# Attention over two heads of one batch per step, K and V in 32 KB runs, in a single-core decode block

## The chip, the cores and the metric

The kernel runs on one core of one Trainium2 chip. The metric is the time of one execution in microseconds of device time; a run is compared by the median of its executions. All data are float32. The whole program is one launch.

## What is computed

A transformer block for one decode step of a batch of two (B = 2, D = 512): a layer norm whose scale, shift and gate come from a condition vector, attention of 32 query heads over 8 cached key and value heads (Dh = 128), of which only the last W = 4096 positions count, and a feed-forward part (F = 1792). Cut to what matters:

```python
mod = (silu(c) @ w_mod).reshape(2, 6, 1, -1)       # six vectors: sa, ca, ga, sb, cb, gb
h = layernorm(x) * (1 + ca) + sa
q = (h @ wq).reshape(B, 1, 32, 128).transpose(0, 2, 1, 3)
k = repeat(k_cache[:, :, Sk - W:, :], 4, axis=1)    # W = 4096, Sk = 32768
v = repeat(v_cache[:, :, Sk - W:, :], 4, axis=1)
p = softmax(einsum("bhqd,bhkd->bhqk", q, k) * 128**-0.5)
o = einsum("bhqk,bhkd->bhqd", p, v)
x = x + ga * (o.transpose(0, 2, 1, 3).reshape(B, 1, 4096) @ wo)
h = layernorm(x) * (1 + cb) + sb
x = x + gb * (silu(h @ w1) @ w2)
```

All of it is read once: 67.1 MB of K and V, 8.4 MB each of wq and wo, 6.3 MB of w_mod, 3.7 MB each of w1 and w2.

## The kernel before

**Memory and loads.** All large data go through one ring in SBUF, `slots` (line 68): 8 slots of 16 KB in each of 128 partitions. `stream(n)` (line 70) hands out the next n neighbouring slots. Every large load is one DMA issued from SP, in the order of the program, and waits there until the slots' last readers are done and what they held has landed. w_mod takes three slots, wq four; then each head of one batch of K or V takes one (2 MiB, 16 KB to a partition), wo two, one and one, and the pieces of w1 and w2 one each. `load_k` and `load_v` (lines 77 and 84) put 32 neighbouring positions of a head into a partition.

**Start.** Matmuls with w_mod give the six vectors (lines 246 and 249), then h and its transpose, then q in two banks of PSUM (`q_ps`, lines 274 to 285), k outermost. Lines 286 to 305 spread q over `qbd`, the blocks that the scores use as weights: `qbd[0]` holds heads 0 to 3 of K, `qbd[1]` heads 4 to 7.

**Attention.** Step h (0 to 7, line 442) treats head h of both batches, with these stages:
- `fetch(h + 1)` issues K of head h + 1, then V of head h, two loads each.
- `keys(h, b, n4)` turns K by transposes of 32 x 32 blocks on VectorE, eight a step, into `kT` (two buffers).
- `scores(h)`: 16 matmuls into one bank, in row blocks by batch b and half c of the 32 positions in a partition; four row blocks of 32, accumulated over j.
- `maxima(h)`: the maximum of each row on VectorE, a matmul that turns the 128 maxima into one row, then the maximum per query head, written to `mrow`.
- `exponentials(h)`: a matmul with `mrow` (bank `bp`) makes the bias, ScalarE the exponentials `pr` and their sums `rowsum`.
- `turn(h)`: transposes `pr`, spreads it with the mask `group` (`zp`), four matmuls with `id4` (bank `pT`), and one ScalarE copy into `ptb`, two buffers of weights for V, with zeros between.
- `weighted(h, b)`: eight matmuls with V of batch b; after the second batch a copy to `ob`. `collect(h)`: four matmuls with `selh` that add the step's result into `o_all`.

`inorder` (line 314) fixes the order within each engine to that of the program. The loop's body (lines 442 to 460) is

```python
fetch(h + 1); keys(h, 0, 0)
turn(h - 1); collect(h - 2); weighted(h - 1, 0)
for n in range(1, 8): keys(h, n // 4, n % 4)
scores(h); maxima(h); exponentials(h)
weighted(h - 1, 1)
```

so V of a step is used one step later.

**End.** The sums are inverted, `o_all` is scaled and brought into `oTn` (lines 475 to 504), wo is applied as its parts land (`acc_o`, `ao`, lines 535 to 556), then the second norm, w1 (`hid`), the gate function and w2 (`acc_yw`, `acc_y`), and the result is stored. `busy` (line 521) issues matmuls into a bank that nobody reads, between these stages.

## Time and profile before

| | |
|---|---|
| median of 3 runs | 236.47 us (236.41 to 236.61) |
| the profiled execution, its own time | 236.49 us |
| its span, first to last instruction | 234.6 us |
| mean TensorE clock granted | 0.874 of full |
| read from HBM | 97.53 MB |
| ScalarE busy, GpSimd busy | 25.4 us, 10.3 us |
| loads of K, of V | 16 and 16, 2048.0 KB each |
| a load of K, of V, from issue to landing (median) | 26.3 us, 27.2 us |

How to read the profile's lines: in a group's line stand the source line, the engine (PE is TensorE, PEld its weight loads, DVE VectorE, ACT ScalarE, POOL GpSimd, SPq the issuing of DMAs from SyncE), the operation, what is written from what, the shapes and the count; then busy time, the mean of one in ns, and the idle time before them with what ended most of it. The time line lists the same by start and duration, with the idle time and what ended it in brackets. A windows row gives for a stretch its length, the busy time and count of PE, PEld, DVE, ACT and POOL, the granted TensorE clock, the DMA engines' busy share and GB/s. The DMA lines count packets, bytes and the share of 16 DMA engines' time that a queue's packets took. A float32 matmul of the program shows as two records. The chain of waits follows the work that ended last back from the end.

### The profile page before, as it was taken

How to read it: one execution, taken by the hardware profiler on the slowest of the kernel's cores; microseconds unless marked ns; L12 is line 12 of the kernel's file. 1: busy time of each engine (PE TensorE's matmuls, PEld its weight loads, DVE VectorE, ACT ScalarE, POOL GpSimd, SP SyncE). 2: the span in 40 equal slices, each digit the busy share in tenths (PEclk: the TensorE clock that was granted, in tenths of full speed). 3: DMA queues.
4: the chain of work that ended last, by engine and by line, in shares of the span. 5: the costliest groups of instructions: out<-in, count | busy, mean ns of one | idle time of the engine just before them, and what ended most of it. 6: DMA issues, size and time to landing. Idle time of an engine off the chain costs nothing.

```text
span 234.6 us, 2609 instructions
## 1 busy us (share of the span) xinstructions
PE 146.2 (62%) x1084; PEld 46.1 (20%) x1084; DVE 113.2 (48%) x175; ACT 25.4 (11%) x56; POOL 10.3 (4%) x30
## 2 busy tenths in 40 slices
PE   0006806917719767675775758746753968499894
PEld 0003201210101121121221112211211222226332
DVE  0124310179369389299398299397298050101130
ACT  2020000010030030030020030120030021003200
POOL 8600000010000000000000000000000000000000
PEclk9999975995965999999998897995995699769998
DMA  7998998999999999999999999999999999999991
GB/s 268 445 540 358 436 458 352 425 425 432 422 439 436 416 439 436 419 439 430 425 436 433 422 433 433 430 427 433 433 425 433 436 439 425 432 418 425 424 415 70
DMA packets 6527, 97.69 MB, mean 416 GB/s; under 512 B 732, under 2 KB 756, under 8 KB 1396
## 3 DMA queue, kind: packets, MB, share of 16 engines
q1 hardware_dynamic: 6492, 97.52, 97.5%
q8 instruction: 8, 0.13, 0.2%
q14 instruction: 3, 0.02, 0.0%
q10 hardware_dynamic: 24, 0.01, 0.0%
HBM read 97.53 MB, written 0.00 MB: 416 GB/s over the span
## 4 chain that ended last, share of the span: by engine, by line
DMA 47%; DVE 30%; PE 17%; ACT 3%; issue 1%; POOL 0%; SPq 0%; POOLq 0%
DVE kT L331 21%; DMA slots<-in_A_wq_dram 15%; DMA slots<-in_A_k_cache_dram 12%; DMA slots<-in_A_wo_dram 12%; PE s L343 8%; DMA slots<-in_B_w_dram 8%; PE q L279 4%; DVE zp L389 3%; PE acc_o L537 3%; DVE xp L387 2%; ACT pr L375 2%; DVE mx L353 1%; PE mT L355 1%; PE bp L371 1%; DVE qT L288 1%
## 5 line engine op out<-in xcount | busy, mean ns | idle before, releaser
L331 DVE STREAM_TRANSPOSE kT<-slots 128x1024 f32<-128x1024 f32 x64 | 73.7, 1210 | 0.3 <-DMA slots<-in_A_k_cache_dram 0.3
L343 PE MATMUL s<-kT,qbd 128*32 128x512 f32 x256 | 48.4, 668 | 13.5 <-DVE kT L331 13.5
L417 PE MATMUL o<-slots,ptb 128*32 128x512 f32 x256 | 37.3, 710 | 11.5 <-DMA slots<-in_A_v_cache_dram 11.0
L353 DVE TENSOR_REDUCE mx<-s 128x1 f32<-128x512 f32 x8 | 5.5, 691 | 36.1 <-PE s L343 36.1
L343 PEld LDWEIGHTS s<-kT,qbd 128*32 128x32 f32 x256 | 11.6, 124 | 51.2 <-DVE kT L331 28.5
L279 PE MATMUL q<-slots,hq_T 128*32 128x512 f32 x64 | 9.4, 756 | 9.1 <-DMA slots<-in_A_wq_dram 9.1
L396 PE MATMUL pT<-zp,id 128*32 128x256 f32 x64 | 5.6, 418 | 13.0 <-DVE zp L389 13.0
L417 PEld LDWEIGHTS o<-slots,ptb 128*32 128x32 f32 x256 | 7.9, 120 | 26.5 <-issue 24.2
L373 ACT COPY bias<-bp 128x1 f32<-128x1 f32 x8 | 1.3, 159 | 107.9 <-PE bp L371 107.9
L213 PE MATMUL mean_a<-mv_a,avg 128*128 128x1 f32 x2 | 0.6, 362 | 18.9 <-DVE avg L118 18.9
L389 DVE TENSOR_TENSOR zp<-xp,group 128x1024 f32<-128x1024 f32 x8 | 9.8, 1225 | 0.2
L537 PE MATMUL acc_o<-slots,oTn 128*32 128x512 f32 x48 | 8.0, 834 | 2.5 <-DMA slots<-in_A_wo_dram 2.5
L288 DVE STREAM_TRANSPOSE qT<-q 128x512 f32<-128x512 f32 x2 | 1.4, 718 | 16.3 <-PE q L279 16.0
L524 PE MATMUL junk<-selh,id 128*32 128x256 f32 x36 | 8.9, 380 | 0.0
L387 DVE STREAM_TRANSPOSE xp<-pr 128x512 f32<-128x512 f32 x8 | 5.7, 711 | 4.7 <-ACT pr L375 4.7
L565 DVE STREAM_TRANSPOSE aoT<-ao 128x128 f32<-128x128 f32 x1 | 0.3, 317 | 14.4 <-PE ao L548 14.4
L355 PE MATMUL mT<-ident,mx 128*1 128x128 f32 x16 | 3.0, 270 | 6.3 <-DVE mx L353 6.3
L432 PE MATMUL o_all<-ob,selh 128*64 128x128 f32 x64 | 5.3, 285 | 1.1 <-ACT ob L426 1.1
L426 ACT COPY ob<-o 128x512 f32<-128x512 f32 x8 | 4.7, 586 | 10.6 <-PE o L417 10.6
L279 PEld LDWEIGHTS q<-slots,hq_T 128*32 128x32 f32 x64 | 2.6, 134 | 16.0 <-issue 16.0
L371 PE MATMUL bp<-negscale,mrow 1*128 1x1 f32 x16 | 3.0, 256 | 4.2 <-DVE mrow L364 4.2
L249 PE MATMUL m_sp<-slots,scT 128*32 128x512 f32 x32 | 5.5, 780 | 0.0
(131 smaller groups left out, 94.0 us busy)
## 6 DMA issues: line engine op xcount, KB each, us to landing
slots<-in_A_k_cache_dram SPq DMA_DIRECT2D x16, 2048.0 KB, 26.3
slots<-in_A_v_cache_dram SPq DMA_DIRECT2D x16, 2048.0 KB, 27.2
slots<-in_w_mod_dram SPq DMA_DIRECT2D x1, 6144.0 KB, 17.2
slots<-in_A_wo_dram SPq DMA_DIRECT2D x1, 4096.0 KB, 27.3
slots<-in_A_wo_dram SPq DMA_DIRECT2D x2, 2048.0 KB, 29.0
slots<-in_B_w_dram SPq DMA_DIRECT2D x2, 1024.0 KB, 21.1
slots<-in_B_w_dram SPq DMA_DIRECT2D x1, 1792.0 KB
slots<-in_B_w_dram SPq DMA_DIRECT2D x2, 896.0 KB, 24.7
```

The costliest lines, as they stand in the source:

```text
L249: nc.tensor.matmul(m_sp[r, :], scT[:, k, :], cd[:, g], start=(k == 0), stop=(k == 3))
L279: nc.tensor.matmul(q_ps[n][32 * g : 32 * g + 32, :], hq_T[:, k, :], wv[:, n, g], start=(k == 0), stop=(k == 3),)
L331: inorder(nc.vector.transpose(kT[h, b][:, :, 8 * n4 : 8 * n4 + 8, :].rearrange("p j n k -> p n j k"), kt[h, b][:, n4 * 1024 : (n4 + 1) * 1 ...
L343: inorder(nc.tensor.matmul(s_ps[h][r : r + 32, :], qbd[h // 4][:, h % 4, b, j, :], kT[h, b][:, j, 16 * c : 16 * c + 16, :], start=(j == 0) ...
L353: inorder(nc.vector.tensor_reduce(mx, s_ps[h], axis=AX.X, op=ALU.max))
L355: inorder(nc.tensor.matmul(mT[0:1, :P], mx, ident, start=True, stop=True))
L387: inorder(nc.vector.transpose(xp, pr[h]))
L389: inorder(nc.vector.tensor_mul(zp, xp[:, None, :, 0:16].to_broadcast([P, 4, 16, 16]), group[:, :, None, None].to_broadcast([P, 4, 16, 16]),))
L396: inorder(nc.tensor.matmul(tp[32 * i : 32 * i + 32, :], id4, zp.rearrange("p a s x -> p (a s) x")[:, :, 4 * i : 4 * i + 4], start=True, st ...
L417: inorder(nc.tensor.matmul(o_ps[h][32 * c : 32 * c + 32, :], ptb[h % 2][:, 256 * b + 32 * w : 256 * b + 32 * w + 32], vt[h, b][:, 512 * w ...
L524: inorder(nc.tensor.matmul(junk[0:32, :256], id4, selh.rearrange("p m y -> p (m y)")[:, :256], start=True, stop=True,))
L537: inorder(nc.tensor.matmul(acc[32 * g : 32 * g + 32, :], oTn[:, q, :], wot[q], start=(q < 4), stop=(q >= 20),))
```

## The change

- Loads: `load_pair(cache, s)` takes two slots and loads heads 2i and 2i + 1 of batch b for step s = 2i + b, in one DMA of 4 MiB. The partitions alternate between the two heads, and each holds 64 neighbouring positions (32 KB). `stream` aligns even requests to their size, so wq moves from slots 3 to 6 to slots 4 to 7, and slot 3 is left out once.
- Steps: still eight, now of two heads (e) of one batch. c is the half of the 64 positions. `scores(s, c)` is a half with eight matmuls whose moving operand takes every other key; `keys(s, c, n4)` likewise.
- `turn` uses the masks `quarter` and `mix`, and `ptb` is filled by two ScalarE copies, scaled by `odd` with 1 or 0 by partition, instead of one copy between fixed zeros. The masks are five small VectorE instructions at the start; the two memsets of `ptb` go.
- Order of a step: the first half of the scores stands at the step's start, on keys that were turned in the step before; half of the next step's first four transposes stand before the maxima and half behind the exponentials. In the last two steps no keys are turned ahead in this way; step 6's `turn` follows it directly, and both of its halves of `weighted` stand behind the exponentials of step 7.
- q: the matmuls go n outermost; `place(0)` fills `qbd[0]` before the loop, `place(1)` fills `qbd[1]` in step 1, all in program order.
- `rx` (for the sums) is made by one multiplication for each batch.

```diff
     def stream(n=1):
         i = turn_of[0]
-        if i % RING + n > RING:
-            i += -i % RING
+        if n % 2 == 0:
+            i += -i % n
...
+    def load_pair(cache, s):
+        i, b = divmod(s, B)
+        t = stream(2)
         nc.sync.dma_start(
-            t, k_cache[b, h, SK - W :, :].rearrange("(p n) d -> p (n d)", p=P)
+            t,
+            cache[b, 2 * i : 2 * i + 2, SK - W :, :].rearrange("e (u n) d -> u e (n d)", u=P // 2),
         )
...
-    for k in range(4):
-        for n in range(2):
+    for n in range(2):
+        for k in range(4):
...
+    def fetch(s):
+        if s < STEPS:
+            kt[s] = load_pair(k_cache, s)
+        if s > 0:
+            vt[s - 1] = load_pair(v_cache, s - 1)
...
+    def scores(s, c):
+        if c == 0:
+            s_ps[s] = bank("A", f"s{s}")
+        i, b = divmod(s, B)
         for j in range(4):
+            for e in range(2):
+                r, h = 64 * e + 32 * c, 2 * i + e
+                inorder(nc.tensor.matmul(
+                    s_ps[s][r : r + 32, :],
+                    qbd[h // 4][:, h % 4, b, j, :],
+                    kT[s, c][:, j, :, e:32:2],
...
-        inorder(nc.scalar.copy(
-            ptb[h % 2]
...
+        for e in range(2):
+            inorder(nc.scalar.activation(
+                ptb[s % 2][:, :, e, :],
+                tp.rearrange("p (w z) -> p w z", z=16),
+                AF.Copy,
+                scale=odd[:, e : e + 1],
+            ))
...
     fetch(0)
+    for n4 in range(4):
+        keys(0, 0, n4)
+    for s in range(STEPS + 1):
+        last, now, more = s > 0, s < STEPS, s < STEPS - 2
         if now:
+            fetch(s + 1)
+            scores(s, 0)
+        if last and s != STEPS - 1:
+            turn(s - 1)
+        if s > 1:
+            collect(s - 2)
+        if s == 1:
+            place(1)
+        if last and s != STEPS - 1:
+            weighted(s - 1, 0)
+        if now:
+            for n4 in range(4):
+                keys(s, 1, n4)
+            scores(s, 1)
+            for n4 in range(2 * more):
+                keys(s + 1, 0, n4)
+            maxima(s)
+            exponentials(s)
+            for n4 in range(2, 2 + 2 * more):
+                keys(s + 1, 0, n4)
+        if s == STEPS - 1:
+            weighted(s - 1, 0)
         if last:
+            weighted(s - 1, 1)
+        if s == STEPS - 2:
+            turn(s)
+            for n4 in range(4):
+                keys(s + 1, 0, n4)
+    collect(STEPS - 1)
```

More of the change, by code (lines that the diff above doesn't have):

```diff
@@ L351, in maxima @@
[L351 to L354 removed]
+            for e in range(2):
+                r, h = 64 * e + 32 * c, 2 * i + e
+                inorder(nc.tensor.matmul(
+                    s_ps[s][r : r + 32, :],
+                    qbd[h // 4][:, h % 4, b, j, :],
+                    kT[s, c][:, j, :, e:32:2],
+                    start=(j == 0),
+                    stop=(j == 3),
+                ))
@@ L441, in adaln_block @@
     fetch(0)
-    for h in range(HKV + 1):
-        last, now = h > 0, h < HKV
+    for n4 in range(4):
+        keys(0, 0, n4)
+    for s in range(STEPS + 1):
+        last, now, more = s > 0, s < STEPS, s < STEPS - 2
         if now:
-            fetch(h + 1)
-            keys(h, 0, 0)
-        if last:
-            turn(h - 1)
-        if h > 1:
-            collect(h - 2)
-        if last:
-            weighted(h - 1, 0)
-        if now:
-            for n in range(1, 8):
-                keys(h, n // 4, n % 4)
-            scores(h)
-            maxima(h)
-            exponentials(h)
-        if last:
-            weighted(h - 1, 1)
-    collect(HKV - 1)
+            fetch(s + 1)
[20 more added lines that the diff above has]
+            weighted(s - 1, 0)
+        if last:
+            weighted(s - 1, 1)
[4 more added lines that the diff above has]
+    collect(STEPS - 1)
     gaT, sbT, cbT = turned(ga, "gaT"), turned(sb, "sbT"), turned(cb1, "cbT")
```

193 lines of the change are left out of this document (93 added, 100 removed).

## The prediction

> **What bounds the kernel now.** I read the page's head and its slices first, then the transfers.
>
> ```profile
> span 234.6 us, 2609 instructions
> PE 146.2 (62%) x1084; PEld 46.1 (20%) x1084; DVE 113.2 (48%) x175; ACT 25.4 (11%) x56; POOL 10.3 (4%) x30
> DMA  7998998999999999999999999999999999999991
> q1 hardware_dynamic: 6492, 97.52, 97.5%
> ```
>
> Packets of one queue fill 97.5% of what 16 DMA engines have in the span, and no slice but the first, the last and two early ones (8) is below 9. TensorE is busy 62% of it and VectorE 48%. The next view cuts the span into three stretches; the last two columns are the DMA engines' busy share and GB/s.
>
> ```profile
> 0.00:1.70 1.70, 0.00 (x0) 0.00 (x0) 0.36 (x4) 0.00 (x0) 1.09 (x8) 1.00 0.00 0
> 1.70:230.60 228.90, 145.52 (x1072) 45.90 (x1076) 112.25 (x169) 25.43 (x56) 9.23 (x23) 0.87 1.00 427
> 230.60:234.60 4.00, 0.71 (x22) 0.23 (x12) 0.58 (x2) 0.00 (x0) 0.00 (x0) 0.84 0.00 1
> ```
>
> So the span is 1.7 us of start, 228.9 us in which the engines never pause (share 1.00), and 4.0 us from the last packet to the end. The chain of waits names other things in its first half, since it follows the compute that was catching up, but from 141.57 us on it is transfers:
>
> ```profile
> 141.57 28.36 DMA slots<-in_A_k_cache_dram
> ...
> 176.62 27.34 DMA slots<-in_A_wo_dram
> ...
> 204.10 7.13 PE acc_o L537 x38
> ...
> 211.25 19.00 DMA slots<-in_B_w_dram
> ...
> 230.29 1.06 PE acc_y L636 x24
> ```
>
> The rule that follows: a change gains only by making the packets themselves shorter, and loses by leaving an engine without a packet, or by making the compute behind the last weights late. The profiled execution took 236.49 us, 1.9 us more than its span and equal to the median of 236.47; my sum starts from 236.5.
>
> **The packets.** The change gives K and V half as many packets of twice the size (32 KB). The trace has packets of 16, 32 and 64 KB. Three stretches of the DMA view, in order: 60 to 160 us (K and V alone, 16 KB), 193.45 to 201.6 us (the first part of wo, 32 KB), 16.94 to 36.33 us (wq, 64 KB, from its first packet to the first of K).
>
> ```profile
> DMA packets 2964, 43.06 MB, mean 431 GB/s; under 512 B 336, under 2 KB 336, under 8 KB 336
> q1 hardware_dynamic: 2961, 43.01, 100.5%
> ```
> ```profile
> DMA packets 113, 3.51 MB, mean 430 GB/s; under 512 B 6, under 2 KB 6, under 8 KB 6
> q1 hardware_dynamic: 113, 3.51, 99.6%
> ```
> ```profile
> DMA packets 144, 8.39 MB, mean 433 GB/s; under 512 B 16, under 2 KB 16, under 8 KB 16
> q1 hardware_dynamic: 144, 8.39, 100.0%
> ```
>
> Those under 512 B only signal completion. 2961 - 336 = 2625 packets of 16 KB in 100 us on 16 engines: one starts 1600 / 2625 = 609.5 ns after the one before it, and lasts 1.005 times that, 612.6 ns; the excess over 100% says that neighbours overlap a little. At 32 KB, 107 packets last 0.996 x 8.15 x 16 / 107 = 1214 ns, 607.0 per 16 KB. At 64 KB, 128 packets in 19.39 us are 2424 ns from start to start, 606.0 per 16 KB. An engine has 32 x 128 / 16 = 256 of the 16 KB packets.
>
> The upper bound goes by durations: (612.6 - 607.0) x 256 = 1.4 us. The lower goes by starts: a fixed part a per packet and a rest b, with a + b = 609.5 and a/4 + b = 606.0, give a = 4.7 ns; 32 KB saves half of it on each 16 KB, 2.35 x 256 = 0.6 us.
>
> I take 0.8 us, nearer to the starts, because with engines that never pause the end follows when packets start and not how long each is shown. The signals, 16 loads instead of 32, are inside these averages.
>
> The Trainium skill, "DMA: Bandwidth & Descriptors", section "Where 436 GB/s comes from", puts the ceiling of 16 ports at 435.2 GB/s; at that rate instead of 430 the 155.8 us of K and V would be 1.9 us shorter. The wq row, at 433 with twice the change's packet size, speaks for less.
>
> **The ring in pairs.** The 8 slots are now handed out two at a time, so a load waits for both. A pair is 4.19 MB, 9.75 us at 430 GB/s; a slot's next load is due three pairs (29.2 us) after its own landing. The durations of one step, from the chain:
>
> ```profile
> 81.68 0.70 DVE mx L353
> ...
> 83.32 0.39 PE bp L371 x2
> ...
> 84.74 0.72 DVE xp L387
> ...
> 86.71 7.92 DVE kT L331 x7
> ```
>
> Half of the next keys' transposes now stand ahead of the maxima on VectorE, so in the bounded state the maxima of step s wait for K of s+1 to land. From that landing: two transposes (7.92 / 7 = 1.13 us apart, 2.3), maxima up to bp 1.6 (81.68 to 83.32), two more transposes 2.3, xp and zp 2.0 (84.74 to 86.71), four transposes 4.5: K is free after 12.7 us, 16 us early. V of s-1, which landed 9.75 us before, goes with the second half of weighted, behind bp and so behind those maxima: 2.3 + 1.6 + 0.4 + 3.64 (eight matmuls at half clock, row below) = 8 us after the landing, 18 us after its own, 11 us early. VectorE's 113.2 us, early work and all, are 14.2 a step, of 19.5. SP issues in order, so a late V holds back the K behind it; the lead of 11 us is the smaller and holds for both. So I cost the order of scores, maxima and transposes, that of the last two steps, the loads issued from SP behind these waits, and the two copies that fill ptb at nothing: what hides them is 11 us of queued packets. One access of TensorE is shown nowhere, the scores' moving operand with a step of two (`e:32:2`). The scores now:
>
> ```profile
> L343 PE MATMUL s<-kT,qbd 128*32 128x512 f32 x256 | 48.4, 668 | 13.5 <-DVE kT L331 13.5
> ```
>
> Its price lies between nothing and twice these 48.4 us. I take nothing, since the operand has as many elements as now; doubled, TensorE's 146.2 us would be 194.6, still under the 228.9 of the transfers.
>
> At the start, K0 waits for w_mod's slots 0 and 1, so for the first three k of its matmuls, instead of having a free slot. Before's K load that waits for the last k, and one of the constants:
>
> ```profile
> 28.29 0.33 SPq L79 DMA_DIRECT2D slots<-in_A_k_cache_dram  x1
> ```
> ```profile
> L114 DVE TENSOR_REDUCE id<-ident 128x32 f32<-128x128 f32 x1 | 0.4, 361 | 0.0
> ```
>
> It was issued at 28.29 us, and wq keeps the engines until 36.33. Five more small constants on VectorE ahead of the moments, at most 0.4 us each, leave 6 of these 8 us. V0 waits for wq's k = 1 of the second half of q; all of q ends at 46.0:
>
> ```profile
> 37.36 8.63 PE q L279 x56
> ```
>
> That is early, since V0 is due at 36.33 + 19.5 = 55.8. Cost: nothing. Splitting q gains nothing either: the matmul of qr0 stands behind the second half's matmuls on TensorE, and K0 as a pair lands only after 36.33 + 9.75 = 46.1.
>
> **The end of attention.** V7 lands as one pair at the time at which its second half does now, and after it this chain remains (before's timeline):
>
> ```profile
> 160.38 3.64 PE L417 MATMUL o<-slots,ptb 128*32 128x512 f32 x16 [4.22 <-DMA slots<-in_A_v_cache_dram]
> ...
> 188.07 0.69 DVE L353 TENSOR_REDUCE mx<-s 128x1 f32<-128x512 f32 x1 [7.01 <-PE s L343]
> ...
> 190.02 1.92 PE L417 MATMUL o<-slots,ptb 128*32 128x512 f32 x16
> ...
> 193.86 0.37 ACT L403 COPY ptb<-pT 128x256 f32<-128x256 f32 x1 [1.24 <-PE pT L396]
> 194.31 3.64 PE L417 MATMUL o<-slots,ptb 128*32 128x512 f32 x32
> ...
> 201.61 0.26 DVE L502 COPY oTn<-oq 128x64 f32<-128x64 f32 x1 [1.26 <-PE oq L499]
> 204.07 0.23 PEld L537 LDWEIGHTS acc_o<-slots,oTn 128*32 128x32 f32 x8 [2.64 <-issue]
> 204.10 2.79 PE L537 MATMUL acc_o<-slots,oTn 128*32 128x512 f32 x12 [2.53 <-DMA slots<-in_A_wo_dram]
> ```
>
> The windows of the two groups of 16 records give the clock that TensorE was granted in them (third column from the right):
>
> ```profile
> 160.38:164.02 3.64, 3.64 (x20) 1.11 (x24) 2.33 (x3) 0.00 (x0) 0.00 (x0) 0.50 1.01 432
> 190.02:191.94 1.92, 1.92 (x17) 0.41 (x16) 0.81 (x3) 0.94 (x3) 0.00 (x0) 1.00 1.05 452
> ```
>
> So they cost 1.92 us at full clock and 3.64 at half. Today oTn is ready at 201.87 and waits 2.2 us for wo. After: K7's first half lands at 169.93 now (the chain above), the pair with the second half at 174.8; eight transposes (9.0 us) after turn's zp, from about 175, and the scores' second half (1.92 to 3.64 us) put the maxima of step 7 between 186.0 and 187.7, some 1.1 us earlier than 188.07. But all of step 6's weighted (3.84 us, not 1.92) now stands between bp and pT, and ptb takes two copies (+0.4). At full clock oTn comes 1.9 + 0.4 - 1.1 = 1.2 us later, at 203.1, with wo landing at 204.07 - 0.8 = 203.3. So the cover of 2.2 us shrinks to 0.2, at no cost.
>
> **Sum:** 236.5 - 0.8 = 235.7.
>
> **Rivals.**
>
> *A late end of attention (slower).* If TensorE is at half clock while step 6's sixteen matmuls run, they take 7.28 us instead of 3.84 and oTn is ready at 203.1 + 3.4 = 206.5, 2.4 us after acc_o's start now. Behind acc_o there are three places where TensorE waits for weights:
>
> ```profile
> 222.30 0.96 PE L588 MATMUL hid<-slots,hT_b 128*32 128x448 f32 x8 [0.28 <-DMA slots<-in_B_w_dram]
> ...
> 227.19 0.16 PEld L624 LDWEIGHTS acc_yw<-slots,uT 128*32 128x32 f32 x8 [0.45 <-DMA slots<-in_B_w_dram]
> ...
> 230.29 0.38 PEld L636 LDWEIGHTS acc_y<-slots,uT 128*32 128x32 f32 x16 [0.34 <-DMA slots<-in_B_w_dram]
> ```
>
> They absorb 0.28 + 0.45 + 0.34 = 1.1 us, so the end is 1.3 us later: 237.8; with half of the matmuls cold, 1.7 us less, nothing is lost. It decides from oTn later than 204.1 + 1.1 = 205.2. For it: TensorE pauses while VectorE turns the keys of step 7, and the first row above shows a start at half clock after such a pause (4.22 us). Against it: acc_o itself ran at half clock before (7.13 us for 38 records where 3.64 for 32 would make 4.3), so a TensorE kept busier may give 2.8 us back.
>
> By the Trainium skill, "TensorE: Matmul & The Clock Gate", section "What's actually happening", the array falls to half clock after an idle window of about 3.4 us; by that the pause before step 7's scores brings this rival on, and the 4.22 us row agrees with it.
>
> *Packets of two heads are slower (slower).* Neighbouring partitions now read from two heads that lie 16 MiB apart, and a source of 64 x 2 rows feeds 128 partitions; no row shows either. The slowest large packets in the trace are those of w_mod, 48 KB each, in the first stretch (1.7 to 16.94 us):
>
> ```profile
> q1 hardware_dynamic: 128, 6.29, 100.4%
> ```
>
> 15.24 x 16 / 128 = 1905 ns, 635 per 16 KB; at that price K and V cost 25.5 x 256 = 6.5 us more: 243. Two engines that get in each other's way throughout would double 156 us: 392. Against it: each packet is still one run of 32 KB into one partition.
>
> The Trainium skill, "DMA: Bandwidth & Descriptors", section "Latency and other measured facts", reports rows a large power of two apart at half rate or less; by that it is the 392. The trace's K and V runs stand 16 KB apart and cannot show it.
>
> *The change doesn't shorten the packets, or the tail eats it (the same).* If a run is moved as two of 16 KB, or the late oTn costs about the 0.8 us: 236.4. For it: the cover behind attention is down to 0.2 us.
>
> **How the numbers follow.** Forecast 0.56 at 235.7, its own range 234.9 to 236.0; the same 0.16; late attention 0.16, from 237 to 237.8; slower packets 0.12, of which 0.05 for the doubled 392 and 0.07 for prices about the 243 of w_mod's. The range of 234.8 to 237.8 leaves out the 0.12 and about 0.05 at the ends. A difference of 0.2% (0.5 us) is about what a measurement of this kernel can tell; faster by more 0.56, within 0.16, slower 0.28.
>
> **What would show it.** The DMA view between 60 and 160 us should have half the packets, about 1215 ns each, 431 to 433 GB/s and a share near 1.00; pauses there, or longer packets, would prove me wrong. The first load of wo should start 0.6 to 1.4 us before 192.12. acc_o should start near 203.5 and wait for wo, or for oTn by less than 1 us; the last matmuls should still wait for weights.

## The result and the profile after

| | before | after |
|---|---|---|
| median of 22 runs each, taken in turn | 236.53 us (236.37 to 236.71) | 237.41 us (236.46 to 238.9) |
| the profiled execution, its own time | 236.49 us | 238.65 us |
| its span | 234.6 us | 236.8 us |
| mean TensorE clock granted | 0.874 | 0.883 |

The ratio is 1.0048, 95% interval 1.0033 to 1.0062: the change made the kernel slower by 0.5% (0.4% by the medians alone), where 235.7 us was forecast. The runs of after also lie 2.4 us apart, those of before 0.3, and the profiled execution of after is 1.2 us above its median, so the traces below show a larger loss than the median does.

The head of the page of after, its DMA queue, and the group of the scores:

```profile
span 236.8 us, 2593 instructions
PE 160.1 (68%) x1084; PEld 51.4 (22%) x1084; DVE 113.6 (48%) x181; ACT 29.1 (12%) x64; POOL 9.5 (4%) x28
q1 hardware_dynamic: 4188, 97.52, 96.0%
L368 PE MATMUL s<-kT,qbd 128*32 128x512 f32 x256 | 67.5, 688 | 15.9 <-DVE kT L355 15.8
```

TensorE has as many instructions as before and 13.9 us more to do with them (146.2 before); the scores take 67.5 us instead of 48.4. The DMA view of after between 60 and 160 us:

```profile
DMA packets 1481, 43.21 MB, mean 432 GB/s; under 512 B 160, under 2 KB 160, under 8 KB 160
q1 hardware_dynamic: 1477, 43.16, 100.1%
```

1477 - 160 = 1317 packets of 32 KB in 100 us on 16 engines: one every 1600 / 1317 = 1215 ns, as forecast. The windows of after, cut near the end of the packets (columns as before: the last two are the DMA share and GB/s):

```profile
1.70:229.80 228.10, 156.32 (x1018) 49.14 (x1022) 112.64 (x175) 28.49 (x63) 8.37 (x22) 0.88 1.00 428
229.80:236.80 7.00, 3.74 (x74) 2.28 (x69) 0.58 (x2) 0.59 (x1) 0.00 (x0) 0.95 0.00 1
```

In windows of 0.02 us the last packet of after ends at 229.9 us, that of before at 230.6. So the transfers end 0.6 to 0.7 us earlier and never pause, but 6.9 us follow them, not 4.0: behind the packets 2.9 us were lost to compute. The chain of waits of after says where that compute comes from:

```profile
128.83 25.93 DMA slots<-in_A_k_cache_dram
154.85 2.37 DVE kT L355 x2
157.23 0.59 DVE mx L378
...
159.55 3.57 PE o L443 x16
163.12 3.61 PE s L368 x13
...
170.73 3.61 PE s L368 x16
174.37 0.70 DVE mx L378
...
179.40 4.54 DVE kT L355 x4
183.99 5.82 PE s L368 x16
...
190.39 3.75 PE s L368 x16
...
208.56 7.05 PE acc_o L580 x48
```

Its last wait for a transfer ends at 154.85 us, with the landing of K of step 6. From there on it is compute, over two whole steps. Before, the compute of the last step still waited for its K until 169.93 us (141.57 + 28.36), and acc_o then for wo. Now, from the time line of after:

```profile
178.17 1.23 DVE L414 TENSOR_TENSOR zp<-xp,quarter 128x1024 f32<-128x1024 f32 x1
179.32 9.12 DVE L355 STREAM_TRANSPOSE kT<-slots 128x1024 f32<-128x1024 f32 x8
183.99 5.82 PE L368 MATMUL s<-kT,qbd 128*32 128x512 f32 x16 [3.80 <-DVE kT L355]
190.32 3.79 PE L368 MATMUL s<-kT,qbd 128*32 128x512 f32 x16
194.17 0.69 DVE L378 TENSOR_REDUCE mx<-s 128x1 f32<-128x512 f32 x1 [5.73 <-PE s L368]
208.23 0.27 DVE L545 COPY oTn<-oq 128x64 f32<-128x64 f32 x1 [1.26 <-PE oq L542]
208.56 4.05 PE L580 MATMUL acc_o<-slots,oTn 128*32 128x512 f32 x20 [0.36 <-DVE oTn L545]
```

oTn is ready at 208.50, 6.6 us later than before, and acc_o no longer waits for wo (2.53 us before) but for oTn. The suspects are in these rows. A half of the scores, 16 records, takes 3.79 us; before, the 32 of step 7 took 4.78 us, and that at a mean clock of 0.76, in this windows row of before:

```profile
183.22:188.00 4.78, 4.78 (x36) 1.21 (x28) 0.00 (x0) 0.00 (x0) 0.00 (x0) 0.76 1.01 428
```

The first half of step 7 takes 5.82 us behind a pause of 3.80 us of TensorE. And the step's chain starts from a load that lands as a whole.

### The profile page after: what moved, and what is told of

It is laid out like the page before. It is cut to its first block, busy times and chain, and to the rows that moved or that the text cites. A ratio compares the mean times of both kernels' runs of the same rounds, so it can differ in the third digit from the quotient of the medians.

```text
span 236.8 us, 2593 instructions
## 1 busy us (share of the span) xinstructions
PE 160.1 (68%) x1084; PEld 51.4 (22%) x1084; DVE 113.6 (48%) x181; ACT 29.1 (12%) x64; POOL 9.5 (4%) x28
## 4 chain that ended last, share of the span: by engine, by line
PE 35%; DMA 35%; DVE 25%; ACT 2%; issue 1%; ACTq 0%; DVEq 0%
DMA slots<-in_A_k_cache_dram 29%; DVE kT L355 16%; PE s L368 14%; DMA x_sp<-in_A_x_dram 6%; PE o L443 5%; PE acc_o L580 3%; PE junk L567 2%; DVE mx L378 2%; DVE zp L414 2%; PE hid L631 1%; PE m_sp L267 1%; PE mT L380 1%; ACT ptb L429 1%; PE m_a L264 1%; PE pT L421 1%
## 5 line engine op out<-in xcount | busy, mean ns | idle before, releaser
L355 DVE STREAM_TRANSPOSE kT<-slots 128x1024 f32<-128x1024 f32 x64 | 74.2, 1212 | 25.3 <-DMA slots<-in_A_k_cache_dram 23.2
L368 PE MATMUL s<-kT,qbd 128*32 128x512 f32 x256 | 67.5, 688 | 15.9 <-DVE kT L355 15.8
L443 PE MATMUL o<-slots,ptb 128*32 128x512 f32 x256 | 35.1, 679 | 2.0 <-ACT ptb L429 1.9
L368 PEld LDWEIGHTS s<-kT,qbd 128*32 128x32 f32 x256 | 16.2, 123 | 64.4 <-issue 49.0
L380 PE MATMUL mT<-ident,mx 128*1 128x128 f32 x16 | 3.7, 317 | 17.2 <-DVE mx L378 17.2
L414 DVE TENSOR_TENSOR zp<-xp,quarter 128x1024 f32<-128x1024 f32 x8 | 9.8, 1226 | 0.2
L429 ACT ACTIVATE ptb<-pT,odd 128x256 f32<-128x256 f32 x16 | 6.7, 472 | 25.1 <-PE s L368 14.3
L421 PE MATMUL pT<-zp,mix 128*32 128x256 f32 x64 | 8.6, 384 | 1.3 <-DVE zp L414 1.3
L580 PE MATMUL acc_o<-slots,oTn 128*32 128x512 f32 x48 | 7.1, 750 | 0.4 <-DVE oTn L545 0.4
L452 ACT COPY ob<-o 128x512 f32<-128x512 f32 x8 | 4.7, 586 | 16.8 <-PE o L443 16.8
L396 PE MATMUL bp<-negscale,mrow 1*128 1x1 f32 x16 | 3.6, 294 | 4.2 <-DVE mrow L389 4.2
L380 PEld LDWEIGHTS mT<-ident,mx 128*1 128x1 f32 x16 | 0.7, 81 | 24.8 <-DVE mx L378 24.8
## 6 DMA issues: line engine op xcount, KB each, us to landing
slots<-in_w_mod_dram SPq DMA_DIRECT2D x1, 6144.0 KB, 17.1
slots<-in_A_wo_dram SPq DMA_DIRECT2D x1, 4096.0 KB, 24.9
```

Source lines behind the costliest of these rows:

```text
L355: inorder(nc.vector.transpose(kT[s, c][:, :, 8 * n4 : 8 * n4 + 8, :].rearrange("p j n k -> p n j k"), kt[s][:, lo : lo + 1024].rearrange(" ...
L368: inorder(nc.tensor.matmul(s_ps[s][r : r + 32, :], qbd[h // 4][:, h % 4, b, j, :], kT[s, c][:, j, :, e:32:2], start=(j == 0), stop=(j == 3),))
L380: inorder(nc.tensor.matmul(mT[0:1, :P], mx, ident, start=True, stop=True))
L414: inorder(nc.vector.tensor_mul(zp, xp[:, None, :, 0:16].to_broadcast([P, 4, 16, 16]), quarter[:, :, None, None].to_broadcast([P, 4, 16, 16 ...
L421: inorder(nc.tensor.matmul(tp[32 * i : 32 * i + 32, :], mix.rearrange("p v e -> p (v e)"), zp.rearrange("p y t x -> p (y t) x")[:, :, 4 * ...
L429: inorder(nc.scalar.activation(ptb[s % 2][:, :, e, :], tp.rearrange("p (w z) -> p w z", z=16), AF.Copy, scale=odd[:, e : e + 1],))
```

## Experiments

Each run stands beside runs of before on the same chip (medians 236.33 to 236.57). "Half clock" is a granted clock of 0.50 in the windows.

### The moving operand, and the order in which keys lie

**plain_operand**: after, with the scores' operand read without the step of two. Each of these matmuls takes keys of both heads for those of one.

```diff
-                    kT[s, c][:, j, :, e:32:2],
+                    kT[s, c][:, j, 16 * e : 16 * e + 16, :],
```

> The changed kernel, with one edit: the scores' moving operand takes 512 neighbouring elements of kT in place of every second one (so each row block sees keys of both heads mixed; the same number of matmuls and elements). Theory 'strided operand' (an operand with a step of two halves the rate of the scores' matmuls, and the end of attention hangs on them): 16 score records take 1.9 us at full clock where they take 3.6 to 3.8, the scores' group falls from 67.5 to about 49 us, oTn is ready near 202 to 204 (208.5 now), the transfers end at about 229.8 as now, and the time is 235.7 (235.2 to 236.2). Theory 'half clock' (TensorE's pauses make it slow): the scores' group stays above 60 us and the time at 237 or more. Theory 'order' (step 6's sixteen matmuls with V behind bp of step 7): scores faster, but oTn later than 205 and the time still above 236.5.

236.41 us (235.55 to 238.03), ratio 1.0004 (0.9989 to 1.002). The group of the scores, over the whole run:

```profile
L368 PE MATMUL s<-kT,qbd 128*32 128x512 f32 x256 | 67.8, 655 | 10.7 <-DVE kT L355 10.7
```

67.8 us, as after (67.5): the step of two is not what made the scores longer. A half at full clock takes 3.61 us instead of 3.77 to 3.79, so the step costs 0.2 us a half. The median is 1.0 us below after's, though the group is no shorter. In the trace the first of these matmuls need only two of four transposes, and the half clock at step 7's scores lasts 3.4 us (181.5 to 184.8), not 6.8. This time fits none of the three theories.

**split_write** and **split_16k**: the transposes themselves put the two heads apart; the second also issues each pair as two DMAs with 16 KB packets.

```diff
-            kT[s, c] = ktp.tile([P, 4, 32, 32], F32, tag="kT", name=f"kT{s}_{c}")
+            kT[s, c] = ktp.tile([P, 32, 4, 2, 16], F32, tag="kT", name=f"kT{s}_{c}")
...
-            kT[s, c][:, :, 8 * n4 : 8 * n4 + 8, :].rearrange("p j n k -> p n j k"),
-            kt[s][:, lo : lo + 1024].rearrange("p (n j r) -> p n j r", j=4, r=32),
+            kT[s, c][:, 8 * n4 : 8 * n4 + 8].rearrange("p n j e q -> p (n j) q e"),
+            kt[s][:, lo : lo + 1024].rearrange("p (m q e) -> p m q e", q=16, e=2),
...
```

> The changed kernel, with the transposes writing the two heads' keys apart (kT as n, j, head, key), so that the scores' operand is runs of 16 elements; everything is computed as before. Theory 'strided operand': as with plain_operand, 235.7, the scores' group about 49 us, provided that the transposes stay at 1.21 us with a write that jumps between two places; if the write costs them, they are above 1.3 us and keys come later by 8 times the excess per step, which the transfers hide up to step 6. Theory 'half clock' or 'order': 237 or more.

> split_write with each pair loaded by two DMAs of 16 KB to a partition in place of one of 32 KB; nothing else. The prediction's packet term: K and V take 0.6 to 1.4 us longer again, the last packets start at about 230.5 instead of 229.8, and the time is 0.8 us above split_write, if split_write is bounded by the transfers. Rival (packet size has no worth): the same time as split_write.

253.89 us (ratio 1.0716) and 251.62 (1.0651). The transposes of split_write:

```profile
L355 DVE STREAM_TRANSPOSE kT<-slots 128x1024 f32<-128x1024 f32 x64 | 114.4, 1914 | 0.5 <-DMA slots<-in_A_k_cache_dram 0.5
```

1914 ns instead of 1212 when each block's columns are written to two places in turn: VectorE bounds both, so they say nothing about packets.

**before_strided**: before, with the step of two in its four-row-block scores.

```diff
-                        kT[h, b][:, j, 16 * c : 16 * c + 16, :],
+                        kT[h, b][:, j, :, c:32:2],
```

> The kernel before, with one edit: the scores' moving operand takes every second key of all 32 columns in place of 16 neighbouring columns (so the two row blocks of a batch hold other keys than V's weights assume; the same number of elements). Theory 'strided operand': the scores' group rises from 48.4 to about 67 us and step 7's sixteen matmuls end 2 to 3 us later; before's cover of 2.2 us ahead of acc_o takes most of it, so 236.5 to 237.5 with oTn between 204 and 206. Theory 'half clock' or 'order': the group stays at 48 to 50 us and the time at 236.5.

238.68 us, ratio 1.0108. The group grew only to 55.5 us (48.4), but each step now waits for all four transposes of a batch (idle 31.2 us ahead of the group, 13.5 before) and runs at half clock behind that wait. Cost and wait can't be told apart here; plain_operand did that.

### The row blocks

Before, eight successive records go to four row blocks of PSUM (`r = 64 * b + 32 * c`). In after's halves c is fixed, so they go to two. **four_blocks** gives each half all four, with matmuls of 256 columns (the matching choice of V's positions in `weighted` isn't shown):

```diff
-                r, h = 64 * e + 32 * c, 2 * i + e
-                inorder(nc.tensor.matmul(
-                    s_ps[s][r : r + 32, :],
-                    qbd[h // 4][:, h % 4, b, j, :],
-                    kT[s, c][:, j, :, e:32:2],
+                for d in range(2):
+                    r, h = 64 * e + 32 * d, 2 * i + e
+                    inorder(nc.tensor.matmul(
+                        s_ps[s][r : r + 32, 256 * c : 256 * c + 256],
+                        qbd[h // 4][:, h % 4, b, j, :],
+                        kT[s, c][:, j, 16 * d : 16 * d + 16, e:32:2],
...
```

> The changed kernel, with each half of the scores spread over all four blocks of 32 output rows (16 matmuls of 256 columns in place of 8 of 512; the four weights blocks for V are picked to match). All of it is computed. Theory 'two blocks' (the halves of the changed kernel write only two of the four row blocks, and TensorE runs four blocks side by side): at full clock a half takes 1.9 to 2.2 us (3.6 to 3.8 now), the scores' busy time falls from 67.5 to 45 to 55 us, oTn comes at 203.5 to 205.5 (208.5 now), and the time is 235.7 to 236.2. Theory 'step of two' (the strided operand alone is what costs): a half stays above 3 us and the time at 237. Theory 'half clock': the halves get shorter, but the time stays above 236.8.

236.89 us (236.73 to 237.21), ratio 1.0014 (1.0005 to 1.0023). A half in step 6, the same half of after, and step 7 with the end of attention (time lines of four_blocks, of after, and of four_blocks again):

```profile
168.20 2.01 PE L369 MATMUL s<-kT,qbd 128*32 128x256 f32 x32
```
```profile
170.55 3.77 PE L368 MATMUL s<-kT,qbd 128*32 128x512 f32 x16
```
```profile
175.22 9.12 DVE L355 STREAM_TRANSPOSE kT<-slots 128x1024 f32<-128x1024 f32 x8
186.48 0.69 DVE L379 TENSOR_REDUCE mx<-s 128x1 f32<-128x512 f32 x1 [2.14 <-PE s L369]
200.74 0.27 DVE L548 COPY oTn<-oq 128x64 f32<-128x64 f32 x1 [1.26 <-PE oq L545]
203.27 3.64 PE L583 MATMUL acc_o<-slots,oTn 128*32 128x512 f32 x16 [2.57 <-DMA slots<-in_A_wo_dram]
```

The same products in 2.01 us instead of 3.77. Four halves of steps 6 and 7 save about 4 x 1.76 = 7.0 us, and oTn is ready at 201.0, 7.5 us earlier; acc_o waits for wo again. The halved rate is the largest part of oTn's delay. Yet the time fell by only 0.5 us. That is what the theory 'half clock' expected, but not for its reason: with attention out of the way, the last packets came late, in these windows of four_blocks (DMA share next to last):

```profile
229.80:230.20 0.40, 0.40 (x21) 0.40 (x17) 0.00 (x0) 0.00 (x0) 0.00 (x0) 1.00 0.10 41
230.20:230.60 0.40, 0.40 (x20) 0.23 (x11) 0.00 (x0) 0.00 (x0) 0.00 (x0) 1.00 0.13 51
230.60:231.00 0.40, 0.39 (x16) 0.29 (x16) 0.00 (x0) 0.00 (x0) 0.00 (x0) 1.00 0.11 41
```

A share of 0.10 to 0.13 is about two of 16 engines, still at work for these 1.2 us.

**four_early**: four_blocks with step 6's first `weighted` between the halves of step 7's scores.

```diff
             for n4 in range(4):
                 keys(s, 1, n4)
+            if s == STEPS - 1:
+                weighted(s - 1, 0)
             scores(s, 1)
...
-        if s == STEPS - 1:
-            weighted(s - 1, 0)
```

> four_blocks, with the first half of step 6's matmuls with V put between the two halves of step 7's scores, as in the steps before, in place of behind the exponentials. Theory 'order' (sixteen matmuls behind bp of step 7 hold up pT): oTn 1 to 1.9 us earlier than in four_blocks, and the time lower by up to 0.5 us where four_blocks is not bounded by the transfers yet. Rival: the eight matmuls only move ahead of the maxima and delay them by as much; the same oTn within 0.5 us.

236.92 us, oTn at 202.7, 1.7 later than four_blocks: the work moved and nothing was gained.

**whole_scores**: after, with `scores(s, 0)` returning at once and both halves in `scores(s, 1)`, so four row blocks again.

```diff
         if c == 0:
             s_ps[s] = bank("A", f"s{s}")
+            return
...
             for e in range(2):
-                r, h = 64 * e + 32 * c, 2 * i + e
+                for c in range(2):
+                    r, h = 64 * e + 32 * c, 2 * i + e
```

> The changed kernel with the halves of the scores put together again behind the second half of the keys, in the order j, head, half, so that four row blocks follow one another (the part 'half of the scores ahead' undone). All of it is computed. Theory 'two blocks': 32 records take 3.6 to 4 us at full clock, as before the change, in place of 7.4; step 7's maxima start at 191 to 193 (194.2 now) and the time is 236 to 237. Theory 'step of two': 32 records stay above 6 us, and the time is above 238 since nothing goes ahead any more.

236.75 us (235.76 to 238.54), ratio 1.0009 (0.9989 to 1.0028). oTn at 206.2, 2.3 us earlier; half clock from 180 to 190 us still takes a part.

### The clock behind the pause

**warm** and **warm_bank**: after, with nine matmuls that nothing reads, queued behind step 6's `turn`, where TensorE waits for the keys of step 7. In warm they go into the bank of `o_all` and disturb what is added up there; in warm_bank they have a bank of their own (the edit of warm_bank, in part):

```diff
         if s == STEPS - 2:
             turn(s)
+            warm = bank("B", "warm")
+            for _ in range(9):
+                inorder(nc.tensor.matmul(
+                    warm[0:32, :256],
+                    id4,
+                    selh.rearrange("p m y -> p (m y)")[:, :256],
...
```

> The changed kernel with nine matmuls that nobody reads in the pause ahead of step 7's first half of the scores (180.2 to 184.0 us), so that TensorE doesn't pause there; nothing is left out. Theory 'half clock': the first half takes 3.8 us in place of 5.8, oTn comes 1.5 to 2 us earlier (206.5 to 207), the time is 236.2 to 236.8. Theory 'two blocks' alone: as the half clock is a smaller part, the time falls by less than 0.5 us.

> The changed kernel with nine matmuls whose result is read by nothing, in a bank of their own, queued on TensorE behind the turn of step 6, so that its wait of 3.8 us for the keys of step 7 is filled. Theory (the late end of the attention is what the change lost, and the half clock behind that wait is what makes it late enough to show): no half clock between 170 and 206 us, the first half of the scores of step 7 takes 3.8 us (5.82), oTn by 206.3 (208.5), the last data packet near 230.0, and 235.75 us, 1.65 below the changed kernel: the transfers bound again. Rival (the loss lies in the halves' slow rate alone, the clock is a by-product): oTn no earlier than 207.5 and 237.0 or more.

warm: 235.75 us (235.69 to 235.96, 5 runs), ratio 0.9967 (0.9955 to 0.9979), below the 236.2 to 236.8 expected. warm_bank: median 235.72, but 12 runs from 235.54 to 238.66, three of them over 238.3, and the ratio is open (0.997 to 1.0028). Its profiled execution is the one of 238.66:

```profile
184.35 3.79 PE L368 MATMUL s<-kT,qbd 128*32 128x512 f32 x16
...
207.56 8.07 PE L589 MATMUL acc_o<-slots,oTn 128*32 128x512 f32 x48 [0.36 <-DVE oTn L554]
```

The first half of step 7's scores is at full clock (3.79, not 5.82) as the theory said, but the half clock came later, from 206.25 us on, under oq and acc_o: 8.07 us, where full clock takes 5.36. So oTn came at 207.5 here, not by 206.3. The mean clock granted in each execution tells the runs apart in the same way: 0.905 to 0.912 in the nine under 236.1 us, 0.892 to 0.899 in the three over 238.3.

**warm_all**: warm_bank with one more such matmul queued ahead of the last `collect` and one ahead of oq, where TensorE pauses for 0.8 us each.

```diff
+    filler(1, "warm_ob")
     collect(STEPS - 1)
...
+    filler(1, "warm_on")
     oq = bank("C", "oq")[:, : B * 32]
```

> The changed kernel with the nine unread matmuls behind the turn of step 6 and one more in each of the two pauses of 0.8 us between the last weighted and oq. Theory (the executions over 237 of the version with nine are those in which acc_o fell to half clock after these pauses, as in its profiled one, 8.07 us from 207.56): acc_o 5.4 us at full clock, 235.7 us and no execution over 236.5. Rival (those pauses are too short to matter): medians and spread as with nine, 235.7 with executions over 237.

235.69 us (235.6 to 235.79, 5 runs), ratio 0.997 (0.9958 to 0.9982). acc_o is at full clock:

```profile
206.90 5.36 PE L595 MATMUL acc_o<-slots,oTn 128*32 128x512 f32 x48 [0.36 <-DVE oTn L560]
```

This version is faster than both kernels, and its time is the forecast's. Five runs without one over 237 us don't show by themselves that the pauses of 0.8 us mattered, since warm's five had none either. The busy time of TensorE speaks for it: of all stretches of 3.41 us that end between 197 and 207 us, the emptiest has TensorE busy for 0.69 of it in warm_all and for 0.51 in warm; in warm_bank it is 0.53 ahead of the fall at 206.25. What such shares do to the clock stands in the last section.

**before_warm**: the same nine matmuls in before, behind `collect(5)` in its last step.

```diff
             collect(h - 2)
+        if h == HKV - 1:
+            warm = bank("B", "warm")
...
```

> The kernel before with the same nine matmuls in the wait of TensorE for V ahead of the last step's scores (5.32 us). Theory (before the change the end of the attention is ahead of the weights by 2.5 us, so an earlier end buys nothing; the transfers bound): oTn earlier by up to 1 us, the wait of acc_o for wo longer by as much, and 236.5 us, within 0.2. Rival (a warm TensorE is worth its microsecond in any version): 235.7 us.

236.34 us, ratio 0.9998 (0.999 to 1.0007). The scores of the last step at full clock:

```profile
181.33 3.64 PE L343 MATMUL s<-kT,qbd 128*32 128x512 f32 x32
```

That is 3.64 us for 32 records over four row blocks, 4.78 without the filling. oq ends 1.3 us earlier and acc_o waits for wo 3.58 us instead of 2.53. Where transfers bind, a warm TensorE is worth nothing.

### The packets by themselves, and the landing of a pair

**warm_16k** (warm_bank) and **after_16k** (after), each with the loads of a pair issued as two DMAs of one half of the positions:

```diff
-        nc.sync.dma_start(
-            t,
-            cache[b, 2 * i : 2 * i + 2, SK - W :, :].rearrange("e (u n) d -> u e (n d)", u=P // 2),
-        )
+        for c in range(2):
+            run = slice(4096 * c, 4096 * c + 4096)
+            nc.sync.dma_start(
+                t[:, run],
+                cache[b, 2 * i : 2 * i + 2, SK - W :, :].rearrange("e (u n) d -> u e (n d)", u=P // 2)[:, :, run],
+            )
```

> The same nine matmuls, and every load of a pair of heads issued as two transfers whose packets are 16 KB, as before the change; the rest as changed. Theory (the smaller number of packets is a gain of its own, 0.8 us by the start to start times of the packets): about 1317 packets of K and V more in the span, the mean start of w1 back near 212.1, the last data packet near 230.8, 236.5 us. Rival (the packets' size is worth nothing, and the 235.7 comes from elsewhere): 235.75, as with 32 KB.

> The changed kernel with every load of a pair issued as two transfers with 16 KB packets, which land one after the other, and nothing else. Theory (the first half's keys land 4.9 us before the pair's second half, so that the chain to the end starts 4.4 us earlier, at the price of the 0.8 us of the packets): first transposes of K(6) at 150.4, oTn between 203 and 205 even at half clock, 236.5 us, no execution over 237.2. Rival (the earlier end in the version with nine matmuls and 16 KB came from the matmuls): oTn at 207 or later, 237.4 us or more.

warm_16k: 236.49 us (236.29 to 237.11). Against warm_all, 235.69, both with attention out of the way, the packets are worth 0.8 us (0.75 when each is taken against before on its own chip, 236.38 and 236.33). after_16k: 236.55 us (236.44 to 236.84), ratio 1.0002 (0.9994 to 1.0011), with no filling at all. Its chain of waits:

```profile
120.43 30.30 DMA slots<-in_A_k_cache_dram
150.82 2.37 DVE kT L357 x2
...
204.84 0.28 DVE oTn L547
205.16 6.05 PE acc_o L582 x38
211.22 19.27 DMA slots<-in_B_w_dram
```

K of step 6 lands 4.0 us earlier (its first half, at 150.82), oTn is ready 3.4 us earlier, with the halved rate and the half clock still there, and the end is bound by transfers again. So the landing of a pair as a whole is the third part of the loss, beside the rate and the clock.

**maxima_first** and **maxima_warm**: after and warm_bank, with the order of the maxima undone.

```diff
-            for n4 in range(2 * more):
-                keys(s + 1, 0, n4)
             maxima(s)
             exponentials(s)
-            for n4 in range(2, 2 + 2 * more):
+            for n4 in range(4 * more):
                 keys(s + 1, 0, n4)
```

> The changed kernel with one part undone: the maxima and exponentials of a step stand ahead of all four transposes of the next keys' first half on VectorE, not behind two of them. Everything else as changed, with no filling of TensorE. Theory (in the step from K(6) to the end the chain of waits begins at the landing of K(6) as a whole pair, 154.8 us, because the maxima of step 5 wait for it through two transposes; without that wait weighted(4), and so the scores of step 6, start up to 3.7 us earlier): scores of step 6 from 160 us (162.9), oTn between 204.5 and 206 (208.5), 235.8 us. Rival (the end is late by the rate of the halves and the half clock alone; the order ahead of the maxima takes nothing): oTn at 208 or later, 237.4 us.

> The version before with nine unread matmuls behind the turn of step 6 as well. Theory: both effects add, oTn at 202 to 204, acc_o waits for wo, 235.7 us in all executions, within 0.3 us of one another (the version with the nine matmuls alone lay between 235.54 and 238.66). Rival (the same place is mended twice): oTn as without them, 235.8 us, with executions over 237.

237.68 us (237.17 to 238.09), ratio 1.005, and 236.56 (235.64 to 236.94). Both miss (235.8 and 235.7 were expected): oTn of maxima_first at 209.4. Its chain of waits shows why:

```profile
140.75 0.70 DVE mx L378
...
142.34 4.54 DVE kT L355 x4
146.92 3.14 PE s L368 x13
...
152.13 1.92 PE o L443 x16
154.06 3.62 PE s L368 x16
157.70 0.70 DVE mx L378
...
174.64 0.70 DVE mx L378
```

The wait for K is gone, but the loop is then one chain of compute, 16.95 us a step (140.75, 157.70, 174.64), and the four transposes stand in it whole. With oTn at 209.4 against 208.5, what the early transposes take off this chain is about what the wait for K puts on, so undoing that order wins nothing.

**long_code**: maxima_first with 64 matmuls of 16 columns, read by nothing, in each of steps 1 to 4, to lengthen the program by as many instructions as four_blocks did.

```diff
+        if 1 <= s <= 4:
+            more_code = bank("B", f"code{s}")
+            for _ in range(64):
+                inorder(nc.tensor.matmul(more_code[0:32, 0:16], id4, id4[:, 0:16], start=True, stop=True))
```

> The version with the maxima first and 256 matmuls of 16 columns, 64 in each of steps 1 to 4, whose results nothing reads. Theory (code packets of 16 KB take one engine's time from the data): 512 instructions more, 10 code packets of q8 in place of 8, the ends of the last load's packets 1.1 to 1.4 us apart (0.6), the last of them 0.9 to 1.1 us later, 236.7 us. Rival (the last packets of the versions over four row blocks were late for another reason): last packets and time as without them, 235.8 us.

246.34 to 246.65 us in three executions, by which the ratio is 1.0422, and 251.09 to 251.62 in three others. The expectation was wrong in its design: the matmuls took 4.19 us a step,

```profile
103.45 4.19 PE L484 MATMUL code<-id 128*32 128x16 f32 x127
```

and 16.8 us of them moved the end by 8.8 us in the first three and by 13.4 in the others (medians, against maxima_first): a chain with little slack took half of them or more. It says nothing on late packets.

**blocks_warm**: four_blocks with the nine matmuls, and twelve ahead of acc_o. **whole_warm**: whole_scores with 17 behind the turn of step 6.

```diff
+    busy(12)
     for q in range(24):
```
```diff
             turn(s)
+            filler(17, "warm")
```

> The version with each half of the scores over all four row blocks, with the nine matmuls behind the turn of step 6 and twelve more of the same ahead of acc_o, so that acc_o runs at full clock too. Theory (its 236.9 us comes from the program's length: 512 instructions more are two code packets of 16 KB more, 10 in place of 8, and the packets of the last load end 1.4 us apart in place of 0.6): oTn near 200.5, acc_o under 7 us, and yet the last data packet near 231.0 and 236.7 to 236.9 us. Rival (the half clock of acc_o frees the ring late and so delays the last loads): last data packet near 230.0, 235.7 us.

> The version with the scores of a step in one piece over all four row blocks, with 17 unread matmuls behind the turn of step 6 (its wait there is 3.21 and 2.59 us, with half clock from 180 to 190). Theory (both causes of the late end are mended at once and no instructions are added to the loop): the scores of step 7 take 3.7 us from 186 us, oTn at 203 to 204, 235.7 us, no execution over 236.5. Rival (the forecast's floor holds only by chance, the last packets come late here as with four row blocks in halves): last data packet near 231, 236.6 us or more.

blocks_warm: 236.83 us (236.52 to 237.02), though oTn came near 201: the last packets still end at 231.0. whole_warm: 237.21 us (236.16 to 238.9), with oTn at 204.8 and acc_o partly at half clock (6.92 us); its last packets end at 231.1, as its rival had it. The clock of acc_o is not what delays the last packets (it is at full clock in blocks_warm). Nor is the number of code packets (queue q8 of the page) alone: four_blocks has ten and blocks_warm eleven, but maxima_warm has eight, as after has, and its last packet ends at 230.9 (229.9 in after, 229.7 in warm_all). Why one or two engines fall behind in these versions stays open.

## Why the prediction was wrong

**The packets: right.** 1215 ns from start to start at 32 KB, 432 GB/s. Their worth is 0.5 us by these starts ((609.5 - 607.5) x 256), 0.6 to 0.7 by the end of the last packet, 0.8 by warm_16k against warm_all; 0.8 was taken. Pairs of heads 16 MiB apart cost nothing; the rival of slower packets fell. The measurement of the Trainium skill, "DMA: Bandwidth & Descriptors", section "Latency and other measured facts", by which partitions' rows 4 or 8 MiB apart move at 103 GB/s and padded ones at 214, does not show in this pattern, where neighbouring partitions alternate between two heads.

**The ring in pairs and the start: right as far as transfers go.** The DMA share is 1.00 throughout. But the 11 us of lead were asked only of the loads. That a pair lands as a whole also starts the compute later, by the 4.0 us of after_16k.

**"I take nothing, since the operand has as many elements as now": right about the step of two (0.2 us a half), wrong about the scores.** The group grew by 19.1 us (48.4 to 67.5). Its bounds of nothing and twice did hold that, but the upper end was dismissed by comparing TensorE's sum, 194.6, with the 228.9 us of the transfers. That sum is no measure: the matmuls stand in a chain of waits that runs on past the last keys, 17.1 us from step 5's maxima to step 6's (157.23 to 174.37).

**The end of attention: the step that failed.** "eight transposes (9.0 us) after turn's zp, from about 175, and the scores' second half (1.92 to 3.64 us) put the maxima of step 7 between 186.0 and 187.7". Two things in it were wrong. It took step 6 as done when K of step 7 lands, and it priced a half of the scores at the rate of four row blocks. Measured: K of step 7 lands near 174.3 us (an estimate: two pairs of 9.75 us behind K of step 6, 154.8), but step 6's own scores and maxima (174.37) are then still under way, so the transposes start at 179.32, 4.3 us late. The first half of the scores, 5.82 us mostly at half clock, and the `collect` behind it end 1.9 us after the last transpose (190.32 against 188.44), and the second half takes 3.79. So the maxima come at 194.17. With the scores over four row blocks the same step holds as forecast: four_blocks has the transposes from 175.22 and the maxima at 186.48.

What stands behind the maxima took 14.3 us to oTn, where the forecast had 16.1 (before's 13.8, and 2.3 for eight more matmuls and a second copy). Those matmuls (196.12 to 199.76) run while VectorE makes zp (until 199.20), for which pT has to wait anyway, and so cost less than their length. "The cover shrinks to 0.2, at no cost" became 6.6 us of delay in oTn and 2.2 us in the profiled execution; wo itself was there at 203.2 (issued at 178.30, 24.9 us to landing), as forecast (203.3).

**The rival that came true: the late end of attention**, given 0.16 and 237 to 237.8 us; 237.41 were measured. Its place and its trigger (TensorE pausing while VectorE turns the keys of step 7) were right, its mechanism only in part. It priced half clock on weighted; it fell on the scores and on acc_o, and the halved rate of the scores was not in it, so that its time fits is partly luck. It named oTn later than 205.2 as the point from which it decides. after_16k reached oTn at 205.1 and was bound by transfers; warm_all at 206.85 was still at the forecast's time, since its acc_o took 5.36 us and not 7.05, as the argument against that rival had it.

**Three causes.** Mending one alone puts oTn at 201.0 (rate), 205.1 (landing) or 206.4 (clock, warm), against 208.5, so the parts can't be added up. The third, the clock, also fits the spread: in the profiled execution of after half clock fell on the scores and on acc_o, and warm_all, where it fell on neither, repeats within 0.2 us in five runs. Where it fell in the other runs of after no trace shows.

## What to carry to other kernels

When the transfers bind, price a change to the compute by the chain that runs from the last landings to the first use of what follows, not by an engine's total: here a new order of the scores' matmuls cost more than all packets gave. Before halving a group of matmuls, look at which row blocks neighbouring records write; the same products over two instead of four took 3.77 us instead of 2.01. And where a chain on TensorE decides the end, look at how busy TensorE is in each stretch of 3.4 us ahead of it, and fill its pauses, even those of 0.8 us.

## What the runs showed of the hardware

**The clock follows a fixed grid, and half a busy window is not enough.** In after it fell to half at 181.48 and 208.80 us, 27.32 = 8 x 3.415 us apart, and stayed there for 6.82 = 2 x 3.41 in the first case. The windows of 3.41 us ahead of a fall, in after (two) and warm_bank, and the one at the same place of warm_all's own grid, where no fall came (PE busy first, clock third from the right):

```profile
178.07:181.48 3.41, 0.81 (x12) 0.19 (x8) 3.41 (x5) 1.43 (x3) 0.00 (x0) 1.00 0.99 425
205.39:208.80 3.41, 1.98 (x20) 1.54 (x24) 0.88 (x3) 0.22 (x1) 0.00 (x0) 1.00 1.00 428
```
```profile
202.84:206.25 3.41, 1.82 (x21) 0.96 (x13) 0.61 (x2) 0.59 (x1) 0.00 (x0) 1.00 1.05 452
```
```profile
202.26:205.68 3.42, 2.71 (x26) 1.22 (x19) 1.01 (x4) 0.59 (x1) 0.00 (x0) 1.00 1.02 436
```

A window with TensorE busy for 0.24, 0.58 and 0.53 of it was followed by half clock, without any pause over 0.8 us in the third; 0.79 kept it. In all 20 profiled executions, from 100 to 235 us, the changes of the clock lie on such a grid of 3.413 us. Laid on it, windows at full clock with a share of 0.41 or less always brought the fall (81 falls in all), those of 0.59 or more never did, and between them it went both ways. Half clock lasted one, two or three windows (22, 41 and 12 times), and ended only behind a window in which TensorE was busy for 0.86 of it or more. The page "TensorE: Matmul & The Clock Gate" of the Trainium skill, section "What's actually happening", has the free-running window of 3413 ns, and the trace agrees; it asks for an idle window, and here a half-busy one was enough. Where the grid lies differs from execution to execution, which fits the spread of after.

**Row blocks.** Sixteen records over two row blocks take 0.24 us each (3.77 us in after at full clock), over four 0.11 (before_warm's 32 in 3.64 us at full clock).

**Transposes that write to two places in turn** took 1914 ns each (split_write), instead of 1212 in after.
